# Staging tiles dealt out by hand, two chunks of attention moved later, and nine loads moved to GpSimd's queue

## Chip, cores and metric

The kernel runs on one core of one Trainium2 chip. The metric is the device time of one execution in microseconds. Before the change the median of 13 runs is 215.76 us (214.9 to 217.86).

In the profile PE is TensorE (PEld its weight loads), DVE is VectorE, ACT is ScalarE, POOL is GpSimd, and SP is SyncE, which issues DMAs here. A trailing q (SPq) means the sequencer's issue of a DMA.

## What is computed

A causal linear attention with a decay per head, in blocks, followed by a two-layer feed-forward network with SiLU. Batch 4, 8 heads, 768 positions, head size 64; 3072 tokens of width 512, hidden width 2048.

```python
# per batch and head, block by block
intra = (q_b @ k_b.T) * Dmask          # lam ** (i - j) where i >= j
out_b = intra @ v_b + (q_b * lam_pow) @ kv_state
kv_state = lam_block * kv_state + (k_b * rev_pow).T @ v_b
# then, on x = all heads side by side, 3072 x 512
h = x @ w_in                           # 512 x 2048
g = h * sigmoid(h)
y = g @ w_out                          # 2048 x 512
```

All inputs are float32; the matmuls run in bfloat16.

## The kernel before

**Tiles.** Tokens are cut into 24 chunks of 128 (six for a batch element) and ten groups of 256 or 384 tokens (`GROUPS`). Attention works by chunk, the network by group. For a chunk, queries and keys are scaled by powers of the decay while they are cast ("prep"), transposed, multiplied to scores, masked, and multiplied with the values; a running state `kv_ps` in PSUM is copied to `kvbd` for the next chunk. Keys and values are spread into block-diagonal tiles (`ktbd`, `vpad`, four of each) by DVE copies (`spread_k`, `spread_v`), so that two heads share one matmul. Chunk c uses buffer c mod 4.

**The start.** Chunks 0 to 3 (as two pairs, 0 and 2) and the up-projection of groups 0 and 1 follow a list written by hand, `ORDER`, whose words are carried out in turn by `table`. `kc`, `qc`, `vc` cast a half of a pair; `tk`, `tq` transpose on PE; `kt`, `qt` copy the transposes out of PSUM; `s` scores, `m` mask, `d` state update, `kv` state copy, `o` output, `x` copy of the output to `xt`, `w` cast of an input-weight piece, `u` and `g` up-projection and SiLU, `z` filler matmuls on a tile of zeros. A letter says which engine does it (A: ACT, D: DVE, P: POOL). Every engine works in the order of the program.

**Loads.** SP issues all large DMAs in program order. At the start these are 12 half pairs of chunks 0 to 3 (into tiles `pair`, six buffers that rotate), then the eight input-weight pieces W0 to W7 as 16 transfers of 256 KB into tiles borrowed from the `kf`, `vf` and `qf` rotations, then six output-weight pieces and the pair of chunk 4's queries into `pair` again, and so on. A later issue waits in SP's queue behind an earlier one.

**From chunk 6 on** keys and queries are transposed by DMA (`dma_t`, L373 and L374, on SP) after POOL's prep (L356 queries, L350 keys), and spread by DVE (L183). `next_prep` does this for the next chunk, and issues the loads of the chunk two further on (`load_c`, L232: queries, keys, values, 256 KB each in runs of 256 B). `piece(c, ...)` calls it until chunk c + 2 is prepared.

**The middle.** After the list, `down0` runs the down-projection of groups 0 and 1 with the attention of chunks 4 and 5 between its parts. Two calls of `next_prep` and the memsets of `clear_halves(0, 1)` (POOL; L198, L199) lie there. Then `stretch` interleaves, by positions between 0 and 1, the up-projection of one group (`ups`), the attention of the next group's chunks (`pieces`: scores, state, output for each) and the down-projection of the group before (`downs`). In the third group's stretch chunks 6 and 7 are placed from 0.2 to 1.15, chunk 6's keys are spread at 0.05, and half of the third group's down-projection comes at 1 to 1.5; the other half lies in the next stretch.

Of the kernel before, what the change touches and what calls it, by code (L numbers as in the profile page):

```python
# [12 lines left out]
BLK = 128  # L13
# [9 lines left out]
LOADS = "K00 Q00 K01 Q01 V00 V01 K20 Q20 K21 Q21 V20 V21 W0 W1 W2 W3 W4 W5 W6 W7"  # L23

ORDER = """
kc:0,0,A,u z:27 tk:0,0,att qc:0,0,D tq:0,0,h kc:0,1,D,s qt:0,0,D wl z:2 tk:0,1,att kt:0,1,A qc:0,1,P kt:0,0,D vc:0,0,D,s
z:4 s:0,0,h,att m:0,0,0,D vc:0,1,A,u tq:0,1,o z:1 d:0 m:0,0,1,D qt:0,1,A z:2 s:0,1,att,att kc:2,0,P,s kv:0,A m:0,1,1,D
m:0,1,0,D tk:2,0,h kt:2,0,D kc:2,1,A,u o:0,0,h,att qc:2,0,P qc:2,1,P x:0,0,A d:1 kv:1,A tq:2,0,o qt:2,0,D tk:2,1,o
kt:2,1,D o:0,1 x:1,1,A z:3 tq:2,1,h qt:2,1,D vc:2,0,A,u vc:2,1,P,s s:2,0,att,o m:2,0,1,D z:4 s:2,1,o,att m:2,0,0,D
m:2,1,1,D x:1,0,A m:2,1,0,D x:0,1,A w:0,1,D d:2 kv:2,A z:28 d:3 w:1,0,D o:2,0,o,att w:0,0,A o:2,1 x:2,0,D w:1,1,D w:2,0,D  # L30
kv:3,A x:2,1,D u:0,0,0,h,h x:3,0,D x:3,1,A w:3,1,D w:2,1,A w:3,0,D u:0,0,1 w:6,0,D g:0,0,1 g:0,0,0 w:5,0,D w:4,1,A
w:4,0,D u:1,1,0,o,o u:1,1,1 g:1,1,1 g:1,1,0 u:1,0,0,h,h u:1,0,1 g:1,0,0 g:1,0,1 w:7,0,D w:6,1,D w:5,1,A w:7,1,D
u:0,1,0,o,o u:0,1,1 u:0,2,0,h,h g:0,1,1 u:0,2,1 g:0,1,0 u:0,3,0,o,o u:0,3,1 g:0,2,0 g:0,2,1 u:1,3,0,h,h g:0,3,0 g:0,3,1
u:1,3,1 g:1,3,0 g:1,3,1 u:1,2,0,o,o u:1,2,1 g:1,2,1 g:1,2,0
# [4 lines left out]
def kernel(  # L39
# [72 lines left out]
    zero = const.tile([128, 256], BF16, name="zero")  # L112
# [33 lines left out]

    def w_piece(which, i, a, b):
        if which == "in":
            c, h = divmod(i, 2)
            return slice(2 * h + a, 2 * h + b), slice(512 * c, 512 * c + 512)  # L150
        return slice(2 * i + a, 2 * i + b), slice(0, DM)

    def load_w(which, *pieces):
        for i in pieces:
            if which == "in":
                for a in range(2):
                    ko, f = w_piece(which, i, a, a + 1)
                    n = 2 * i + a
                    tag = "qf" if n >= 12 else ("kf", "vf")[a]
                    t = io.tile([128, 1, 512], F32, name=tag, tag=tag, bufs=4 if tag == "qf" else 6)  # L160
                    nc.sync.dma_start(out=t, in_=w_in_r[:, ko, f])
                    wtmp[which, i, a] = t
            else:
                ko, f = w_piece(which, i, 0, 2)
                t = io.tile([128, 2, 512], F32, name="pair", tag="pair", bufs=6)
                nc.sync.dma_start(out=t, in_=w_out_r[:, ko, f])
                wtmp[which, i] = t

    def cast_w(which, i, e="D", part=None):
        a, b = (0, 2) if part is None else (part, part + 1)  # L170
        ko, f = w_piece(which, i, a, b)
        if which == "in":
            move(e, w_in_bf[:, ko, f], wtmp[which, i, part])
        else:
            move(e, w_out_bf[:, ko, f], wtmp[which, i][:, a:b, :])
# [30 lines left out]
    cell = {}  # L206
    start = 0
# [11 lines left out]
    def load_pair(src, c, dst, parts=((0, H),)):  # L219
        b, blk = divmod(c, NB)  # L220
        for lo, hi in parts:
            if c not in dst:
                dst[c] = io.tile([128, H, 2, D], F32, name="pair", tag="pair", bufs=6)
            nc.sync.dma_start(out=dst[c][:, lo:hi].rearrange("p h r d -> p h (r d)"),  # L224
                              in_=src[b, lo:hi, blk * BLK:(blk + 2) * BLK, :].rearrange("h (p r) d -> p h (r d)", r=2))
# [3 lines left out]
    def load_1(src, c, tag, bufs):  # L229
        b, blk = divmod(c, NB)  # L230
        t = io.tile([128, H, D], F32, name=tag, tag=tag, bufs=bufs)
        nc.sync.dma_start(out=t, in_=src[b, :, blk * BLK:(blk + 1) * BLK, :].rearrange("h s d -> s h d"))  # L232
        return t
# [12 lines left out]
    def pair_op(c, a, e, table, src, dst):  # L246
        hs = slice(4 * a, 4 * a + 4)
        src, dst = src[:, hs].rearrange("s h r d -> s r h d"), dst[:, :, hs, :]
# [8 lines left out]
    def op_c(raw, tiles, name, forward=False):  # L257
        def run(c, a, e, s="s"):
            if c not in tiles:
                tiles[c] = nat.tile([128, 2, H, D], BF16, name=name, tag=name, bufs=2)  # L260
# [3 lines left out]
    def op_t(src, name):  # L264
        def run(c, a, tag):
            tp = psum.tile([128, 2, 2, BLK], BF16, name=name, tag=tag, bufs=NBUF[tag], padded_shape=[128, 4, 2, BLK])
            for r in range(2):
                for p in range(2):
                    h = 4 * a + 2 * p
                    nc.tensor.transpose(tp[:, r, p, :], src[c][:, r, h:h + 2, :], ident)  # L270
# [3 lines left out]
    def op_tc(dst, name, of):  # L274
        def run(c, a, e):
            if c not in dst:
                dst[c] = nat.tile([128, 2, NP, BLK], BF16, name=name, tag=name, bufs=2)
            move(e, dst[c][:, :, 2 * a:2 * a + 2], cell.pop((of, c, a)))
# [4 lines left out]
    def op_s(c, a, *tags):  # L283
        sps = [psum.tile([128, 2, 2, 2, 64], F32, name="sp", tag=t, bufs=NBUF[t]) for t in tags]
        for r in range(2):
            for p in range(2):
                for j, x in ((0, 0), (1, 1), (0, 1), (1, 0)):
                    nc.tensor.matmul(sps[j][half[x], r, p], lhsT=ktp[c][half[j], r, 2 * a + p, half[x]],
                                     rhs=qtp[c][half[j], :, 2 * a + p, half[x]], start=True, stop=True)
# [8 lines left out]
    def op_o(c, a, *tags):  # L298
        if a == 0:
            for x, t in enumerate(tags):  # L300
                op_[c + x] = psum.tile([128, NP, 2, 64], F32, name="op", tag=t, bufs=NBUF[t])
        for x in range(2):
            if c + x > 0:
                for p in range(2):
                    nc.tensor.matmul(op_[c + x][:, 2 * a + p], lhsT=kvb[c + x][:, 2 * a + p, :],
                                     rhs=qtp[c][:, :, 2 * a + p, half[x]], start=(a == 0 and p == 0),
                                     stop=False, skip_group_check=True)
        for r in range(2):
            for p in range(2):
                for x, j in ((0, 0), (1, 1), (0, 1), (1, 0)):  # L310
                    nc.tensor.matmul(op_[c + x][half[j], 2 * a + p], lhsT=vp[c][half[x], r, 4 * a + 2 * p + j, :],
                                     rhs=ss_[c, a, j][half[x], r, p], start=(c + x == 0 and a == 0 and r == 0 and p == 0),
                                     stop=(r == 1), skip_group_check=True)

    def op_x(c, a, e):
        g, x = divmod(c, 2)
        if g not in xt:
            xt[g] = xpool.tile([128, KO_IN, GROUPS[g]], BF16, name="xt", tag="xt", padded_shape=[128, KO_IN, 512])
        ps = slice(2 * a, 2 * a + 2)
        move(e, xt[g].rearrange("d p (r x w) -> d p r x w", r=2, x=2)[:, ps, :, x, :], op_[c][:, ps])  # L320

    def op_d(c):
# [4 lines left out]
        for r in range(2):  # L327
            for p in range(NP):
                for j in range(2):
                    nc.tensor.matmul(kv[half[j], p, half[j]], lhsT=kp[c0][half[x], r, 2 * p + j, :],  # L330
                                     rhs=vp[c0][half[x], r, 2 * p + j, :], start=(c == 0 and r == 0 and p == 0), stop=True,
                                     skip_group_check=True)
# [3 lines left out]

    qpairs = {}
# [117 lines left out]
    def copy_kv(c, e="D"):  # L455
        if c % NB == NB - 1:
            return
        kv, kvs = kvps[c // NB], kvbd[c % NKV]
        for j in range(2):
            rows = slice(64 * j, 64 * j + 64)  # L460
            move(e, kvs[rows, :, rows], kv[rows, :, rows])
# [110 lines left out]
    def ffn2(g, mt, kos, tag="o"):  # L572
# [7 lines left out]
        if kos[-1] == KO_OUT - 1:  # L580
# [4 lines left out]
            if g < 2:  # L585
                dst = out[gstart[g]:gstart[g] + 256, :].rearrange("(q r) d -> q r d", r=2)[:, mt, :]
# [20 lines left out]
    for word in LOADS.split():  # L607
        if word[0] == "W":
            load_w("in", int(word[1]))
        else:  # L610
            a = int(word[2])
            src, dst = {"Q": (q, rawq), "K": (k, rawk), "V": (v, vraw)}[word[0]]
            load_pair(src, int(word[1]), dst, ((4 * a, 4 * a + 4),))
    load_w("out", *range(6))
    load_q(4)
    load_k(4), load_k(5)
    load_w("out", 6, 7)
    load_v(4), load_v(5)
    load_c(6)
    load_c(7)  # L620

    def op_u(g, b, h, *tags):
        for i, tag in zip((2 * b, 2 * b + 1), tags):
            ffn1_open(g, i, tag)
        for i in (2 * b, 2 * b + 1):
            ffn1_mm(g, i, range(2 * h, 2 * h + 2))  # L630

    def op_g(g, b, i):
        ffn1_close(g, 2 * b + i)
# [4 lines left out]
    def op_z(n):  # L638
        if 0 in kvps:
            for i in range(n):  # L640
                nc.tensor.matmul(kvps[0][half[0], NP - 1, half[1]], lhsT=zero[:, half[0]], rhs=zero[:, half[0]],  # L641
                                 start=False, stop=True, skip_group_check=True)
        else:
            wt = psum.tile([128, NP, BLK], F32, name="warm_ps", tag="kv", bufs=1)
            for i in range(n):
                nc.tensor.matmul(wt[:, 0:2], lhsT=zero[:, :BLK], rhs=zero, start=True, stop=True)
# [7 lines left out]
    for word in ORDER.split():  # L654
        name, _, args = word.partition(":")
        table[name](*[int(a) if a.isdigit() else a for a in args.split(",") if a])

# [4 lines left out]
    def next_prep():  # L662
        c = state["prepped"]
        if c < NCHUNK:
# [4 lines left out]
            if loads:  # L669
                load_c(loads.pop(0))  # L670
# [3 lines left out]
    for i in range(6):  # L674
        cast_w("out", i)
    for i in range(NKV):
# [28 lines left out]
    next_prep()  # L705
    down0(3, 0)
    st_o(5)
    next_prep()
# [36 lines left out]
    def stretch(*parts):  # L745
# [3 lines left out]
        for _, _, _, (fn, *args) in sorted(units, key=lambda u: u[:3]):  # L749
            fn(*args)  # L750

    stretch((ups(2), 0, 1), ([(vcast, 6)], 0.0, 0.1), ([(spread_k, 6)], 0.05, 0.05), ([(spread_v, 6)], 0.3, 0.3), (pieces(3), 0.2, 1.15),
            (downs(2, range(1)), 1, 1.5))
    for g in range(3, len(GROUPS)):
        parts = [(ups(g), 0, 1), (pieces(g + 1), *((0.1, 0.95) if g == 3 else (0, 0.85)))]
        parts.append((downs(g - 1, range(1 if g == 3 else 0, nch[g - 1])), 0, 1))
# [34 lines left out]
```

## Time and profile before

| | us |
|---|---|
| median of 13 runs | 215.76 |
| the profiled execution | 215.65 |
| its span on the core | 213.9 |
| PE busy | 203.1 (95%) |
| DVE busy | 116.6 |
| ACT busy | 98.4 |
| POOL busy | 53.4 |

The span runs from the first instruction to the last; 1.75 us of the profiled execution's time lie around it. Busy time is the union of an engine's instructions, without DMA issues. The granted TensorE clock is full in all slices. The views used below are the list of waits (who waited for whom, total, number of times, longest), the timeline (start, duration, engine, line, what was written from what, count; the idle time before and what ended it in brackets) and the groups of instructions by line.

### The profile page before, as it was taken

Reading aid. Unit: us, or ns where it says so; the run is one execution under the profiler, and the core shown is the slowest. Engines: PE = TensorE matmul, PEld = TensorE weight load, DVE = VectorE, ACT = ScalarE, POOL = GpSimd, SP = SyncE. Lnnn points to the kernel's source line nnn. Section 1 sums busy time; section 2 is a strip of 40 time slices with the busy share of each in tenths; the row PEclk is TensorE's granted clock in tenths of the full one; section 3 lists DMA queues with packets and bytes.
Section 4 is the critical chain, followed back from the end, with each engine's and each line's share of the span. In section 5 each row is a group of like instructions: output and inputs, shape, how many; then the busy total and the mean of one; then the engine's idle time right before and its main releaser. Section 6 shows DMA issues by size and latency. Waiting matters only on the chain.

```text
span 213.9 us, 4591 instructions
## 1 busy us (share of the span) xinstructions
PE 203.1 (95%) x1808; PEld 135.2 (63%) x1831; DVE 116.6 (54%) x263; ACT 98.4 (46%) x186; POOL 53.4 (25%) x66
## 2 busy tenths in 40 slices
PE   7679999999799999999999999999999999999994
PEld 6467886556677777776665655556655565566654
DVE  3787447597785679854992785345461351110121
ACT  3973863415463564545555445445445334423210
POOL 6360002449433334321333332212000000000000
PEclk9999999999999999999999999999999999999999
DMA  4999999989899999989888999858411011011112
GB/s 113 334 364 326 394 405 270 316 195 199 195 285 204 223 201 193 213 204 202 174 223 196 235 207 182 196 165 174 124 49 52 2 49 54 0 49 49 52 49 98
DMA packets 95670, 38.58 MB, mean 180 GB/s; under 512 B 81056, under 2 KB 88608, under 8 KB 95648
## 3 DMA queue, kind: packets, MB, share of 16 engines
q1 hardware_dynamic: 95504, 38.29, 70.1%
q8 instruction: 14, 0.23, 0.5%
q14 instruction: 8, 0.07, 0.1%
q10 hardware_dynamic: 144, 0.00, 0.0%
HBM read 27.27 MB, written 6.29 MB: 157 GB/s over the span
## 4 chain that ended last, share of the span: by engine, by line
PE 88%; SPq 3%; DVE 2%; DMA 2%; issue 1%; POOL 1%; ACT 1%; POOLq 0%
PE o_ps L578 36%; PE h_ps L552 19%; PE h_ps L529 18%; PE op L507 5%; PE sp L476 3%; SPq L224 3%; DMA pair<-in_q_dram 2%; PE kv_ps L452 2%; PE o_part L595 2%; DVE ktbd L183 1%; DVE xt L183 1%; POOL vp L253 0%; PE kv_ps L641 0%; POOL qb L253 0%; ACT kvbd L179 0%
## 5 line engine op out<-in xcount | busy, mean ns | idle before, releaser
L578 PE MATMUL o_ps<-w_out_bf,g 128*128 128x512 bf16 x345 | 87.9, 379 | 1.2
L578 PEld LDWEIGHTS <-g 128*128 128x128 bf16 x368 | 35.0, 98 | 30.8
L556 ACT ACTIVATE g<-h_ps 128x384 bf16<-128x384 f32 x64 | 31.4, 491 | 46.6 <-PE h_ps L552 46.1
L552 PE MATMUL h_ps<-xt,w_in_bf 128*128 128x384 bf16 x256 | 50.6, 326 | 0.0
L529 PE MATMUL h_ps<-xt,w_in_bf 128*128 128x256 bf16 x384 | 47.2, 273 | 0.7 <-ACT w_in_bf L179 0.7
L534 ACT ACTIVATE g<-h_ps 128x512 bf16<-128x512 f32 x48 | 27.8, 596 | 33.2 <-PE h_ps L529 33.0
L529 PEld LDWEIGHTS <-w_in_bf 128*128 128x128 bf16 x384 | 36.4, 98 | 7.9 <-ACT w_in_bf L179 1.1
L582 DVE COPY ob<-o_ps 128x512 f32<-128x512 f32 x23 | 15.9, 691 | 44.1 <-PE o_ps L578 44.0
L356 POOL TENSOR_TENSOR qb<-qf,lam_fwd 128x512 bf16<-128x512 f32 x18 | 18.9, 1053 | 68.1 <-DMA qf<-in_q_dram 64.3
L552 PEld LDWEIGHTS <-w_in_bf 128*128 128x128 bf16 x256 | 23.7, 98 | 17.2
L483 DVE TENSOR_TENSOR ss<-sp,mask 128x512 bf16<-128x512 f32 (+1 forms) x40 | 21.0, 566 | 14.6 <-PE sp L476 14.4
L387 DVE COPY vpad<-vb 64x256 bf16<-64x256 bf16 x72 | 25.3, 351 | 1.6
L350 POOL TENSOR_TENSOR kb<-kf,lam_bwd 128x512 bf16<-128x512 f32 x20 | 20.9, 1048 | 1.4 <-DMA kf<-in_k_dram 0.9
L183 DVE CAST kvbd<-kv_ps 64x256 bf16<-64x256 f32 x32 | 13.5, 421 | 9.7 <-PE kv_ps L452 9.4
L515 ACT ACTIVATE xt<-op 128x512 bf16<-128x512 f32 x20 | 11.9, 597 | 12.7 <-PE op L507 12.0
L183 DVE COPY ktbd<-kn 64x512 bf16<-64x512 bf16 x36 | 14.3, 396 | 5.0 <-DMA kn<-kb 4.6
L476 PEld LDWEIGHTS <-ktbd 128*128 128x128 bf16 x160 | 9.4, 98 | 5.5 <-DVE ktbd L183 2.3
L476 PE MATMUL sp<-qt,ktbd 128*128 128x128 bf16 (+1 forms) x160 | 10.3, 207 | 1.8 <-DVE ktbd L183 1.8
L179 ACT ACTIVATE vb<-vf 128x512 bf16<-128x512 f32 x18 | 11.2, 622 | 0.0
L507 PE MATMUL op<-ss,vpad 128*128 128x128 bf16 (+1 forms) x160 | 10.3, 207 | 0.0
L507 PEld LDWEIGHTS <-vpad 128*128 128x128 bf16 x160 | 8.9, 98 | 0.3
L183 DVE CAST w_out_bf<-pair 128x1024 bf16<-128x1024 f32 x7 | 5.5, 780 | 4.7 <-DMA pair<-in_moe_w_out_dram 4.7
(83 smaller groups left out, 119.7 us busy)
## 6 DMA issues: line engine op xcount, KB each, us to landing
out_dram<-ob SPq DMA_DIRECT2D x23, 256.0 KB, 3.4
kf<-in_k_dram SPq DMA_DIRECT2D x20, 256.0 KB, 4.0
vf<-in_v_dram SPq DMA_DIRECT2D x20, 256.0 KB, 4.3
qf<-in_q_dram SPq DMA_DIRECT2D x18, 256.0 KB, 3.3
pair<-in_moe_w_out_dram SPq DMA_DIRECT2D x8, 512.0 KB, 7.7
kf<-in_moe_w_in_dram SPq DMA_DIRECT2D x6, 256.0 KB, 5.4
vf<-in_moe_w_in_dram SPq DMA_DIRECT2D x6, 256.0 KB, 5.6
pair<-in_k_dram SPq DMA_DIRECT2D x4, 256.0 KB, 4.5
```

Source lines behind the costliest of these rows:

```text
L183: nc.vector.tensor_copy(dst, src)
L350: VG[e].tensor_tensor(kb, rawk.pop(c).rearrange("s (p j) d -> s p j d", j=2), decay(lam_bwd, c % NB), op=AL.mult)
L356: nc.gpsimd.tensor_tensor(qb, rawq.pop(c).rearrange("s (p j) d -> s p j d", j=2), decay(lam_fwd, c % NB), op=AL.mult)
L387: nc.vector.tensor_copy(vh[64 * j:64 * j + 64, :, h, j, :], vb[64 * h:64 * h + 64, :, j, :])
L476: nc.tensor.matmul(sp[:, p, :], lhsT=lhsT, rhs=qt[:, p, a:], start=True, stop=True)
L483: VG[e].tensor_tensor(ss, sp, m[:, None, :n].to_broadcast([128, 4, n]), op=AL.mult)
L507: nc.tensor.matmul(dst, lhsT=lhsT, rhs=rhs, start=(i == 0), stop=(i >= len(terms) - NP), skip_group_check=True)
L529: nc.tensor.matmul(hps[g, i][:, a:a + 256], lhsT=w_in_bf[:, ko, m * 128:(m + 1) * 128], rhs=xt[g][:, ko, :], start=(ko == 0 and u == 0), s ...
L534: nc.scalar.activation(gg.rearrange("p u n -> p (u n)"), hps[g, i], AF.Silu)
L552: nc.tensor.matmul(hp[:, a:z], lhsT=w_in_bf[:, ko, m * 128:(m + 1) * 128], rhs=xt[g][:, ko, a:z], start=(ko == 0 and a == 0), stop=(ko == ...
L556: nc.scalar.activation(gg, hp[:, :n], AF.Silu)
L578: nc.tensor.matmul(o, lhsT=gt[g, ko][:, mt * BLK:(mt + 1) * BLK], rhs=w_out_bf[:, ko, :], start=(ko == 0), stop=(ko == KO_OUT - 1))
```

## The change

Five things change together.

1. *Staging.* The rotating `pair` tiles become six tiles dealt out in turn by `next_pair`. Input-weight pieces 0 to 5 are loaded as one transfer of 512 KB into them, pieces 6 and 7 into two `kf` and two `vf` tiles. Their loads are no longer issued all together after the inputs: a list `later` issues each as soon as the words of `ORDER` that read its tile are in the program, so that on SP they stand behind the waits for those casts.
2. *The list.* `ORDER` is new. Chunk 2's second half is attended after the up-projection has begun; the state update and its copy can be done by halves (`d:2,0`). Fillers are not instructions in a tile of their own: after the first ones, `z` leaves a number that the next `s`, `o` or `u` writes into its own PSUM tile ahead of its matmuls, with up to 512 columns each.
3. *Layout and width.* Groups 0 and 1 share one tile `xall`, in the order of the tokens; from the second quarter of the hidden width on, their up-projection is done together with 512 columns. The state update takes two heads in one matmul. The stores of groups 0 and 1 are plain rows.
4. *Chunks 6 and 7.* Both are prepared and transposed before the last quarter of `down0`, the loads of chunks 8 and 9 follow after that, and their attention moves from 0.2..1.15 to 0.8..1.9 of the third group's stretch, with the whole down-projection of that group from 1 to 2.
5. *Queue.* The loads of chunks 8, 9 and 10 are issued by GpSimd and not by SP.

The core of the diff:

```diff
-LOADS = "K00 Q00 K01 Q01 V00 V01 K20 Q20 K21 Q21 V20 V21 W0 W1 W2 W3 W4 W5 W6 W7"
+LOADS = "K00 Q00 K01 Q01 V00 V01 K20 Q20 K21 Q21 V20 V21"
 ORDER = """
+kc:0,0,D,u z:20 tk:0,0,h qc:0,0,D kt:0,0,A wl z:8 tq:0,0,o kc:0,1,D,s qt:0,0,A z:2 tk:0,1,h qc:0,1,D z:3 tq:0,1,o
+s:0,0,h,att vc:0,1,A,u vc:0,0,D,s d:0 kt:0,1,D m:0,0,1,D m:0,0,0,D qt:0,1,A kv:0,A s:0,1,att,att qc:2,0,P z:2 o:0,0,h,o
+kc:2,0,A,u m:0,1,0,D m:0,1,1,D x:1,0,D d:1 qc:2,1,P tk:2,0,att tq:2,0,h x:0,0,A kt:2,0,D o:0,1,att,att tq:2,1,o
+kc:2,1,A,u tk:2,1,h qt:2,0,A x:1,1,D x:0,1,D kt:2,1,D vc:2,0,P,s s:2,0,o,h kv:1,A d:2,0 qt:2,1,A vc:2,1,P,s z:2
+s:2,1,att,att m:2,0,0,D m:2,0,1,D kv:2,0,A d:2,1 w:0,1,D kv:2,1,D m:2,1,1,D w:1,1,D o:2,0,h,att m:2,1,0,D w:0,0,A
+u:0,0,0,o,o x:2,0,A d:3 w:1,0,A kv:3,A x:3,0,D u:0,0,1 g:0,0,1 w:2,0,D o:2,1,att,att x:3,1,D x:2,1,A g:0,0,0 w:2,1,D
...
+    pairs = [const.tile([128, 2 * H * D], F32, name=f"pair{i}") for i in range(6)]
...
+            ko, f = w_piece(which, i, 0, 2)
+            t = next_pair().rearrange("p (k f) -> p k f", k=2)
+            nc.sync.dma_start(out=t, in_=(w_in_r if which == "in" else w_out_r)[:, ko, f])
...
+        e = nc.gpsimd if c in (8, 9, 10) else nc.sync
+        e.dma_start(out=t, in_=src[b, :, blk * BLK:(blk + 1) * BLK, :].rearrange("h s d -> s h d"))
...
+        for m in ms:
+            for ko in range(2 * h, 2 * h + 2):
+                nc.tensor.matmul(hps["m", m], lhsT=w_in_bf[:, ko, m * 128:(m + 1) * 128], rhs=xall[0][:, :, ko, :],
+                                 start=(ko == 0), stop=(ko == KO_IN - 1))
...
+        while later and not later[0][2]:
+            load_w(*later.pop(0)[:2])
...
     st_d(5)
-    next_prep()
+    next_prep(0)
+    next_prep(2)
     down0(3, 0)
     st_o(5)
-    next_prep()
     clear_halves(0, 1)
     down0(3, 1)
...
-    stretch((ups(2), 0, 1), ([(vcast, 6)], 0.0, 0.1), ([(spread_k, 6)], 0.05, 0.05), ([(spread_v, 6)], 0.3, 0.3), (pieces(3), 0.2, 1.15),
-            (downs(2, range(1)), 1, 1.5))
+    stretch((ups(2), 0, 1), ([(vcast, 6)], 0.0, 0.1), ([(spread_k, 6)], 0.5, 0.5), ([(spread_v, 6)], 0.6, 0.6),
+            (pieces(3), 0.8, 1.9), (downs(2, range(2)), 1, 2), ([(next_prep,)], 0.6, 0.6))
     for g in range(3, len(GROUPS)):
         parts = [(ups(g), 0, 1), (pieces(g + 1), *((0.1, 0.95) if g == 3 else (0, 0.85)))]
-        parts.append((downs(g - 1, range(1 if g == 3 else 0, nch[g - 1])), 0, 1))
+        if g > 3:
+            parts.append((downs(g - 1, range(nch[g - 1])), 0, 1))
         stretch(*parts)
```

The argument of `next_prep` is the number of chunks whose loads it issues after preparing one.

## Prediction

> **What bounds the kernel now.** I read the page's busy row first: PE is busy for 203.1 of 213.9 us, so time is won only by taking idle time or work out of PE, or lost by making PE wait. The rate tells that the busy time is real: 111 matmuls of 256 columns run from 21.82 to 33.95 us, 0.109 us each, and four of 512 columns take 0.86 us in the chain. The list of waits of PE (total, times, longest) is short:
>
> ```profile
> PE sp L476 <- DVE ktbd L183: 1.8, 1, 1.8
> PE tk L270 <- ACT kp L179: 1.6, 1, 1.6
> ...
> PE kv_ps L641 <- ACT kvbd L179: 0.9, 1, 0.9
> PE h_ps L529 <- ACT w_in_bf L179: 0.7, 1, 0.7
> PE tk L270 <- POOL kp L253: 0.4, 1, 0.4
> ```
>
> One wait, 1.8 us, lies in the dense part: the scores of chunk 6. The others lie before 22 us. The timeline shows the 1.8 us and what stands in front of it (start, duration, engine):
>
> ```profile
> 49.94 0.95 POOL L198 MEMSET ktbd<- 128x1024 bf16 x1
> ...
> 51.92 2.83 DVE L183 COPY ktbd<-kn 64x512 bf16<-64x512 bf16 x2
> ...
> 54.81 0.51 PE L476 MATMUL sp<-qt,ktbd 128*128 128x128 bf16 x8 [1.78 <-DVE ktbd L183]
> ```
>
> The two copies that spread chunk 6's keys take 2.83 us beside POOL's memsets (a pair takes 0.59 at 58.73), and PE stands until 54.81. After that PE is never late, but by little. The SP timeline says why: SP issues transposes, loads and stores one behind the other, without a gap:
>
> ```profile
> 46.99 1.48 SPq L373 DMA_TRANSPOSE qt<-qb  x1
> 48.57 1.21 SPq L374 DMA_TRANSPOSE kn<-kb  x1
> 49.83 0.57 SPq L232 DMA_DIRECT2D qf<-in_q_dram  x1
> 50.46 0.68 SPq L232 DMA_DIRECT2D kf<-in_k_dram  x1
> 51.24 0.66 SPq L232 DMA_DIRECT2D vf<-in_v_dram  x1
> 51.99 0.86 SPq L570 DMA_DIRECT2D out_dram<-ob  x1
> 52.95 1.24 SPq L373 DMA_TRANSPOSE qt<-qb  x1
> ```
>
> A chunk costs SP 2.6 us of transposes and 2.1 us of loads. The spread of chunk 10 ends at 78.36 and its scores start at 78.42; for chunk 14 it is 101.83 and 102.22. So a gain ahead of these chunks stays only if their keys come earlier too.
>
> **The start (order, wide matmuls, staging).** The up-projection starts at 18.97 now. In the new order it follows `o:2,0` and the casts of the first weight piece. POOL gets four tiles of chunk 2: the second query half landed at 12.43 (its row starts on the DMA), then 1.04 each: 13.47, 14.51, 15.55. State update `d:2,1` follows at 15.6, and `o:2,0` ends near 16.5. The first weight piece was cast at 16.24 and 16.73; DVE is free of chunk 2's masks at about 15.8, ACT at 15.4, so I put both casts' end at 16.9 and the first up-projection at 17.0. Behind it stand 32 matmuls of 256 columns (3.5 us), 48 of 512 (10.4) and the attention that was moved behind the start (`d:3`, `o:2,1`: 1.2 from their rows of 0.44 and 0.82): the end is 32.0 instead of 33.95, **1.9 us** earlier. Width alone gives 96 x 0.109 - 48 x 0.215 = 0.1 of this.
>
> The weight loads must now wait for the casts that empty their staging tile, the last on `vc:2,1` (15.55). It costs nothing while earlier loads are in flight: pieces 0 to 4 are issued by 13.5, and the trace moves such a piece in about 1.3 us behind inputs that land until 13.9, so DMA has work until 20. Without that cover each late piece would hold the weights behind it in SP's queue. Fewer fillers (37 units of 256 columns, against 34 and 37 tiny ones) take nothing from the sum; they ran in waits.
>
> Then a DMA is late next: the last output-weight piece lands at 40.49 (ACT idle 5.25 us for it), its cast takes 1.06 and the query copy behind it 0.54, so chunk 4's scores can't start before 42.1; PE would be there at 41.55. That leaves **1.35 us**: the third group starts at 51.12 - 1.35 = 49.75.
>
> **Chunks 6 and 7 later.** Their scores move from 0.2 of the third group to 0.89 of it, 6.1 us in, at 55.9. The keys had landed by 51.92, so the **1.78 us** go. Both chunks now lie between eight units of the down-projection, which are only brought forward from the next stretch. Possible gain: 1.35 + 1.78 + rounding = 3.2 us. Next due, by counting units of 0.87 (up), 0.86 (down) and 1.1 (a chunk's attention): chunk 8 at 66.6, chunk 9 at 71.2, chunk 10 at 75.0.
>
> **Loads 8 to 10 from GpSimd.** SP loses 9 issues of 0.57 to 0.68, some 6 us, which is why its transposes of chunks 8 to 10 need not be late. POOL gets them in its own row of work: prep 6, prep 7, six loads, the four memsets, prep 8, three loads, prep 9, prep 10. Prep 7 ends at 50.0 (it waits for its landing at 47.95). Let one issue hold POOL for t. Memsets (four starts 0.89 apart, 3.7 with the last) and prep 8 (2.1) end at 55.8 + 6t; three loads and prep 9 end at 57.9 + 9t; SP's transposes of chunk 9 take 2.6, load 11 takes 2.1, then the transposes of chunk 10: 1.3 to the second issue, 2.4 to its landing (its median), 0.6 spread. **Chunk 10 is ready at 66.9 + 9t and due at 75.0.** Chunks 8 (60.1 + 6t against 66.6) and 9 (62.2 + 9t against 71.2) are parts of the same loss. Change: -3.2 + (9t - 8.1), the bracket not below 0. Zero at t = 1.26.
>
> The trace has no DMA issued by POOL. Lower bound: SP's issue of the same load, 0.57 (full gain; POOL need not be slower). Upper: the longest issue of such a load, 3.19 (+17.4). Nearest are POOL's own passes: 1.04 for one 128x512 tile; a transfer has 1024 pieces of 256 B to describe, on a reading and a writing side, so one pass to two, 1.04 to 2.08. I take 1.5 as an estimate between these: 9 x 1.5 - 8.1 = 5.4, and -3.2 + 5.4 = +2.2.
>
> DVE copies held up beside POOL show a second price: the copies `ktbd<-kn` have a median of 291 ns and a maximum of 1782. The Trainium skill, "SBUF — State Buffer", section "SBUF: two separate sides", says that GpSimd and a two-port DVE copy lock each other out for a whole instruction, and that a DMA issued from GpSimd can't write its descriptors meanwhile; that would make t longer, no row here shows it. "DMA: Bandwidth & Descriptors", "Specifications", gives about 1 us to the first byte by GpSimd and 0.6 by sync; if 1 us were all of t, the estimate by that page would be -2.3. Its section "Issuing engines are not separate DMA queues" says that other engines save only issue time; here issue time is what SP lacks, so the rule doesn't refute the change, but it names no other gain.
>
> **Rivals.**
> 1. *Forecast, 0.37:* t from 1.33 to 2.2, POOL's queue becomes the bound for chunks 8 to 10; 216.3 to 224.
> 2. *A cheap issue, 0.33:* t up to 1.2. At 0.57 chunk 10 is ready at 72.0 and all 3.2 us stay, 212.5; at 1.04 1.3 us are lost, 213.8. For it: POOL is 25% busy and idles up to 5 us before a prep. Against it: SP's hardware already needs 0.57.
> 3. *A dear issue, 0.21:* t above 2.2: at 2.4 +10.3, 226; at 3.19, 233.
> 4. *Break-even, 0.09:* t near 1.26, or the change doesn't do what it says: the start gains nothing because the weights decide it as before (DVE waited for them until 23.69), or fewer fillers slow the transposes. Then 1.78 is the whole gain and due times come 1.35 later; below t = 1.05 the time is 214.0, above it the sum is as before, since the chain of chunk 10 doesn't move with PE. So a wrong first half moves little.
>
> **Numbers.** The profiled execution took 215.65 with a span of 213.9, so 1.75 lie around it, which I keep; the median of the runs is 0.11 higher. 215.65 + 2.2 + 0.1 = 218.0. The likeliest case's own range is 216.3 to 224. Range of eighty per cent: from the full gain, 212.4, to t = 2.4, 226.0. A measurement can tell some 0.3% from no change; faster (rival 2 and a little of 4) 0.34, same 0.08, slower 0.58.
>
> **What would show it.** Right: PE's wait list has no wait for `ktbd` at chunk 6, the down-projection starts near 32, and there are new waits of `sp` for `ktbd` between 66 and 82, with POOL solid from 48 to about 73. POOL's issue rows give t directly. Wrong: rows of POOL near 0.6 to 1.0 (faster), a first up-projection at 18 or later, or spreads that wait for DVE rather than for prep.

## The result and the profile after

The changed kernel takes **218.14 us** (median of 11 runs, 216.95 to 219.61); the kernel before, run beside it, 215.66. The ratio is **1.0119, 95% interval [1.0092, 1.0146]**. All ratios leave out, on both sides, runs over 1.5% above the fastest of their kernel. The profiled execution took 217.72 with a span of 216.0, against 215.65 and 213.9. Lines of the code have moved: the scores are L492, the output L523, the mask L499, the up-projection L545 (512 columns wide: L645), the down-projection L594, DVE's moves L187, the spread of the values L401, POOL's preps L370 and L364, its memsets L202 and L203.

The list of waits of PE (total, times, longest):

```profile
PE op L523 <- DVE ss L499: 2.1, 1, 2.1
PE sp L492 <- DVE ktbd L187: 2.1, 3, 1.4
...
PE o_ps L594 <- ACT g L654: 0.7, 1, 0.7
...
PE h_ps L545 <- DVE xt L187: 0.6, 1, 0.6
```

One wait for `ktbd` has become three, and there is a new one for the masks. PE's timeline says at which chunks (start, duration; the wait in brackets):

```profile
57.80 0.51 PE L492 MATMUL sp<-qt,ktbd 128*128 128x128 bf16 x8 [1.41 <-DVE ktbd L187]
...
63.22 0.61 PE L523 MATMUL op<-ss,vpad 128*128 128x128 bf16 x8 [2.08 <-DVE ss L499]
...
65.85 0.51 PE L492 MATMUL sp<-qt,ktbd 128*128 128x128 bf16 x8 [0.30 <-DVE ktbd L187]
71.59 0.50 PE L492 MATMUL sp<-qt,ktbd 128*128 128x128 bf16 x8
76.21 0.50 PE L492 MATMUL sp<-qt,ktbd 128*128 128x128 bf16 x8
79.95 0.50 PE L492 MATMUL sp<-qt,ktbd 128*128 128x128 bf16 x8
...
91.19 0.51 PE L492 MATMUL sp<-qt,ktbd 128*128 128x128 bf16 x8 [0.36 <-DVE ktbd L187]
```

Chunks 6 and 7 are late, the very chunks that were moved to be early. Chunks 8, 9 and 10 (71.59, 76.21, 79.95), whose loads POOL issues, wait for nothing. DVE's timeline shows where the time of chunk 6 is:

```profile
50.93 6.82 DVE L187 COPY ktbd<-kn 64x512 bf16<-64x512 bf16 x2
57.78 4.66 DVE L401 COPY vpad<-vb 64x256 bf16<-64x256 bf16 x4
62.47 1.02 DVE L499 TENSOR_TENSOR ss<-sp,mask 128x512 bf16<-128x512 f32 x2
```

The keys were there in time, since the copy began at 50.93 and PE got to the scores at 56.39. But the two key copies take 6.82 us (median of all such copies 0.29 each), the four value copies 4.66 (0.22 each). The first key copy alone ran from 50.93 to 56.70, one value copy for 2.35 from 58.98 to 61.33. The masks stand behind them in DVE's queue, and so the output at 63.22. That order is new: in the kernel before, the masks of chunk 6 (55.32) came ahead of its value copies (56.26), and the fourth part put the values first. Now POOL's row over the same time:

```profile
50.28 0.88 POOL L246 DMA_DIRECT2D qf<-in_q_dram  x1
51.16 0.88 POOL L246 DMA_DIRECT2D kf<-in_k_dram  x1
52.03 0.88 POOL L246 DMA_DIRECT2D vf<-in_v_dram  x1
52.91 0.97 POOL L202 MEMSET ktbd<- 128x1024 bf16 x1
...
55.59 0.97 POOL L203 MEMSET vpad<- 128x1024 bf16 x1
56.51 1.09 POOL L370 TENSOR_TENSOR qb<-qf,lam_fwd 128x512 bf16<-128x512 f32 x1
...
60.39 0.88 POOL L246 DMA_DIRECT2D vf<-in_v_dram  x1
61.29 1.06 POOL L370 TENSOR_TENSOR qb<-qf,lam_fwd 128x512 bf16<-128x512 f32 x1
```

The row has no gap. The first copy ends at 56.70, just after the last memset (56.56), the long value copy at 61.33, just after the last issue (61.27). The loads themselves cost POOL 0.88 to 1.06 each, which is the t of the prediction.

**The account** is of the two profiled executions. A wait costs 0.16 more than the list says, because the modelled duration of the eight matmuls before a dense stretch (0.51) is that much longer than the time to the next start (57.80 to 58.15, 0.35). The third group starts 1.00 earlier (50.12 against 51.12); the old wait saves 1.78 + 0.16 = 1.94; the new ones cost 1.57 + 2.24 + 0.46. Sum +1.33; measured at the scores of chunk 10, 79.95 - 78.42 = +1.53. With chunk 12's 0.52 it is +1.85; measured at chunk 13, 97.96 - 95.91 = +2.05, which stays to the end (span +2.1). Some 0.2 before chunk 10 is not assigned.

### The profile page after: what moved, and what is told of

It reads as the page before. It is cut to its first block, busy times and chain, and to the rows that moved or that the text cites. A ratio compares the mean times of both kernels' runs of the same rounds, so it can differ in the third digit from the quotient of the medians.

```text
span 216.0 us, 4342 instructions
## 1 busy us (share of the span) xinstructions
PE 203.8 (94%) x1677; PEld 127.8 (59%) x1700; DVE 123.4 (57%) x267; ACT 98.7 (46%) x185; POOL 61.0 (28%) x74
## 4 chain that ended last, share of the span: by engine, by line
PE 83%; DVE 7%; issue 2%; DMA 2%; ACT 2%; SPq 2%; DVEq 0%
PE o_ps L594 34%; PE h_ps L568 19%; PE h_ps L545 11%; PE h_ps L645 5%; DVE ktbd L187 5%; PE op L523 5%; PE sp L492 3%; DMA pair<-in_v_dram 2%; PE o_part L609 2%; SPq L237 2%; PE kv_ps L466 2%; DVE vpad L401 1%; PE kv_ps L344 1%; ACT kvbd L183 1%; ACT qtp L183 1%
## 5 line engine op out<-in xcount | busy, mean ns | idle before, releaser
L594 PE MATMUL o_ps<-w_out_bf,g 128*128 128x512 bf16 x346 | 88.1, 379 | 1.8 <-ACT g L654 0.7
L594 PEld LDWEIGHTS <-g 128*128 128x128 bf16 x368 | 34.9, 98 | 31.8 <-issue 1.0
L545 PE MATMUL h_ps<-xt,w_in_bf 128*128 128x256 bf16 x288 | 36.0, 273 | 0.6 <-DVE xt L187 0.6
L370 POOL TENSOR_TENSOR qb<-qf,lam_fwd 128x512 bf16<-128x512 f32 x18 | 18.8, 1047 | 61.9 <-DMA qf<-in_q_dram 61.9
L568 PEld LDWEIGHTS <-w_in_bf 128*128 128x128 bf16 x256 | 23.7, 98 | 17.2
L550 ACT ACTIVATE g<-h_ps 128x512 bf16<-128x512 f32 x36 | 21.4, 597 | 27.3 <-PE h_ps L545 27.1
L499 DVE TENSOR_TENSOR ss<-sp,mask 128x512 bf16<-128x512 f32 (+1 forms) x40 | 21.0, 566 | 17.1 <-PE sp L492 16.8
L545 PEld LDWEIGHTS <-w_in_bf 128*128 128x128 bf16 x288 | 27.1, 98 | 6.1 <-issue 0.5
L187 DVE COPY ktbd<-kn 64x512 bf16<-64x512 bf16 x36 | 23.7, 658 | 0.4
L401 DVE COPY vpad<-vb 64x256 bf16<-64x256 bf16 x72 | 21.3, 296 | 1.6
L364 POOL TENSOR_TENSOR kb<-kf,lam_bwd 128x512 bf16<-128x512 f32 x20 | 21.8, 1091 | 1.6 <-DMA kf<-in_k_dram 1.6
L187 DVE CAST kvbd<-kv_ps 64x256 bf16<-64x256 f32 (+1 forms) x34 | 14.0, 413 | 9.7 <-PE kv_ps L466 9.4
L492 PEld LDWEIGHTS <-ktbd 128*128 128x128 bf16 x160 | 9.3, 98 | 6.3 <-DVE ktbd L187 3.3
L492 PE MATMUL sp<-qt,ktbd 128*128 128x128 bf16 (+1 forms) x160 | 10.3, 207 | 2.2 <-DVE ktbd L187 2.1
L523 PE MATMUL op<-ss,vpad 128*128 128x128 bf16 (+1 forms) x160 | 10.4, 207 | 2.1 <-DVE ss L499 2.1
L523 PEld LDWEIGHTS <-vpad 128*128 128x128 bf16 x160 | 8.9, 98 | 2.8 <-issue 1.7
L645 PE MATMUL h_ps<-xt,w_in_bf 128*128 128x512 bf16 x48 | 10.5, 379 | 0.0
```

The costliest lines, as they stand in the source:

```text
L187: nc.vector.tensor_copy(dst, src)
L364: VG[e].tensor_tensor(kb, rawk.pop(c).rearrange("s (p j) d -> s p j d", j=2), decay(lam_bwd, c % NB), op=AL.mult)
L401: nc.vector.tensor_copy(vh[64 * j:64 * j + 64, :, h, j, :], vb[64 * h:64 * h + 64, :, j, :])
L492: nc.tensor.matmul(sp[:, p, :], lhsT=lhsT, rhs=qt[:, p, a:], start=True, stop=True)
L499: VG[e].tensor_tensor(ss, sp, m[:, None, :n].to_broadcast([128, 4, n]), op=AL.mult)
L523: nc.tensor.matmul(dst, lhsT=lhsT, rhs=rhs, start=(i == 0), stop=(i >= len(terms) - NP), skip_group_check=True)
```

## The experiments

All ratios are to the kernel before, run on the same chip in the same set.

**First set: what holds the copies?** The theory: POOL's unbroken row. The rivals: SP or the landing of the keys, and POOL's queue being late for chunks 8 to 10.

`e1_loads_on_sp`: the change without its fifth part.

```diff
-        e = nc.gpsimd if c in (8, 9, 10) else nc.sync
-        e.dma_start(out=t, ...)
+        nc.sync.dma_start(out=t, ...)
```

> The changed kernel with the nine loads of chunks 8 to 10 back on SP; POOL keeps the four memsets. Held copies (a DVE copy from SBUF to SBUF can't run while POOL works without a gap, as from 47.5 to 61.3 us in the changed kernel): POOL is done with the memsets near 51.1, so the two key copies of chunk 6 end before 52, the waits of 1.41 and 2.08 us at chunk 6 and of 0.30 at chunk 7 go, and the time is 218.1 - 4.3 = 213.8 or a little less. Late queue (what the prediction held: POOL reaches the preps of chunks 8 to 10 too late): the rows of the changed kernel show its issues at 0.9 us, so the queue costs nothing and putting the loads back gives 218, at most 0.5 less. Late data (the new start makes the data of chunks 6 and 7 late): 218, the waits stay.

Measured: 215.47 (12 runs), ratio 0.9957 [0.9916, 0.9998]. The row of memsets now lies from 47.84 to 51.47, before the keys are spread, and DVE's timeline of this run has

```profile
51.42 0.58 DVE L187 COPY ktbd<-kn 64x512 bf16<-64x512 bf16 x2
52.03 0.94 DVE L400 COPY vpad<-vb 64x256 bf16<-64x256 bf16 x4
```

So copies of the same form are short again, and chunk 6 waits for nothing. Chunk 10's scores start at 76.10, 2.3 earlier than before the change. But two new waits follow, at chunks 11 and 12, the time misses the 213.8 of the theory, and at chunk 13 (95.77) 0.1 of the gain is left:

```profile
83.67 0.51 PE L491 MATMUL sp<-qt,ktbd 128*128 128x128 bf16 x8 [1.06 <-DVE ktbd L187]
89.00 0.51 PE L491 MATMUL sp<-qt,ktbd 128*128 128x128 bf16 x8 [0.78 <-DVE ktbd L187]
```

So the fifth part is what holds the copies. In this run its relief of SP is missed too: without it, chunks 11 and 12 are late. SP transposes the keys of chunk 11 only at 78.67, after a set of loads and a store, and they land 4.3 us later, those of chunk 12 at 85.70, 2.6 us. Whether they are late in every such run, `e4_sp_and_clear_on_dve` puts in doubt.

`e2_clear_on_dve`: the loads stay on GpSimd, the four memsets go to DVE.

```diff
-            nc.gpsimd.memset(ktbd[i], 0.0)
-            nc.gpsimd.memset(vpad[i], 0.0)
+            nc.vector.memset(ktbd[i], 0.0)
+            nc.vector.memset(vpad[i], 0.0)
```

> The changed kernel with the loads of chunks 8 to 10 on POOL, but the four memsets done by DVE (4 x 0.5 us, from about 50.5 to 52.5). Held copies: POOL's unbroken row shrinks by 3.6 us; the first key copy ends behind the sixth issue near 53, the second near 54, so the wait at the scores of chunk 6 (due 56.2) goes, while the value copies may still be held by the issues for chunk 10, 0 to 1.5 us at chunk 6's output; 214.5 (213.8 to 216). If it is the DMA issues alone that hold the copies: as here, 214.5. If it is the memsets alone: 213.8 and no copy longer than 0.5 us. Late data: 218.

Measured: six runs, one of 214.17 and five of 218.17 to 219.67, so there is no ratio; the trace is of a run of 218.66. In it the first key copy lasts from 52.75 to 54.02, to the end of the six issues (53.90): issues alone hold a copy too. The second takes 2.10, beside two preps. Chunks 6 and 7 don't wait, but chunk 8 does, for 3.02, because its keys' transpose landed 13.2 us after its issue (56.52 to 69.7) in place of 2.4. DVE's timeline names that as the cause of its idle time:

```profile
69.79 0.89 DVE L187 COPY ktbd<-kn 64x512 bf16<-64x512 bf16 x2 [4.55 <-DMA kn<-kb]
```

Whether the run of 214.17 escaped that, no trace shows.

`e3_chunk6_on_act`: chunk 6's spreads on ACT.

```diff
-                move_k("D", c, j, kn)
+                move_k("A" if c == 6 else "D", c, j, kn)
```

(and so for the values)

> The changed kernel, all of POOL's work as it is, but the six copies that spread chunk 6's keys and values run on ACT instead of DVE (some 0.6 us for a key copy, 0.4 for a value copy, 2.8 in all, in a stretch where ACT idles 0.28 us per SiLU). Held copies: ACT isn't held by POOL, so the waits of 1.41 and 2.08 us go; up to 1 us may come back where SiLU is late for PE; 214.5 (213.8 to 215.5). Late data: the copies on ACT wait as long as those on DVE did, 217.5 to 218.5. Late queue: 218.

Measured: 217.26 against the 214.5 expected, ratio 1.0065 [1.0029, 1.0100]. Chunk 6's scores no longer wait for keys. But chunk 7's copies, still DVE's, now meet POOL's second row (key copies from 62.26, 3.40 us), its scores wait 1.44, and PE waits 1.7 for SiLU results behind the copies on ACT. The hold moved with the place, as it must if the row makes it.

`e4_sp_and_clear_on_dve`: the edits of `e1_loads_on_sp` and `e2_clear_on_dve` together.

> The changed kernel with the loads of chunks 8 to 10 on SP and the four memsets on DVE, so that POOL has only preps. Held copies: all waits of chunks 6 and 7 go, 213.8 as with the loads on SP alone, within 0.5 (the memsets then cost 2 us of DVE where it has slack). Late data or late queue: 218. If SP's queue is what the loads were moved away from, new waits for keys appear at chunks 8 to 10 and the time is above 214.5.

Measured: 215.72, ratio 0.9965 [0.9921, 1.0008], with runs from 212.94 to 216.57; the interval reaches 1, and the 213.8 expected is missed. In the profiled one (214.15) the only waits for `ktbd` are 0.33 (chunk 9) and 0.26 (chunk 14), and chunk 10's scores are at 76.55. Chunks 11 and 12 don't wait here, though the loads are on SP as in `e1_loads_on_sp`: the keys of chunk 11 are transposed at 78.16 and land in 2.6. How much of that is the memsets' place and how much differs from run to run isn't shown.

**Second set: the form of the copy, and each part alone.**

`e5_two_input`: the changed kernel, chunks 6 and 7 spread by DVE with another operation of the same result (the core of the edit; it is done for these two chunks alone).

```diff
-nc.vector.tensor_copy(dst, src)
+nc.vector.tensor_tensor(dst, src, src, op=AL.max)
```

> The changed kernel, but the spreads of chunks 6 and 7 (keys and values) are DVE operations with two inputs, the larger of a tile and itself, in place of copies with one input; the values written are the same, the engine and the place in its queue too. Theory (POOL's unbroken row of issues and memsets holds a DVE copy of SBUF to SBUF in its one-input form): the first of chunk 6's key operations no longer takes 5.77 us but under 1, PE's waits of 1.41 and 2.08 at chunk 6 and 0.30 at chunk 7 go, and the time is 218.1 - 3.5 = 214.6; 2.2 of these should show at chunk 10, whose scores then start near 77. Rival (whatever DVE writes to SBUF is held while POOL is busy, in any form): the operations still take over 3 us and the time stays within 217 to 219. Rival 2 (the keys themselves are late and the copy's duration is only where it shows): the waits stay, and the operations begin later.

Measured: ratio **0.9938 [0.9887, 0.9989]**, from four runs of 214.12 to 215.71; the profiled one took 214.22. Five others took 217.40 to 218.88, and no trace tells why; a late landing as in `e2_clear_on_dve` isn't excluded there. In the profile no score waits for `ktbd` (chunk 7's output waits 0.43 for its masks), and chunk 10's scores are at 76.45 (expected near 77). DVE's timeline:

```profile
51.39 0.84 DVE L411 TENSOR_TENSOR ktbd<-kn 64x512 bf16<-64x512 bf16 x2
52.27 1.20 DVE L411 TENSOR_TENSOR vpad<-vb 64x256 bf16<-64x256 bf16 x4
...
61.20 2.34 DVE L411 TENSOR_TENSOR vpad<-vb 64x256 bf16<-64x256 bf16 x4
```

The first two lines run beside the six issues (48.63 to 54.06 here), which are part of the row that held the copy for 5.77 us, and are not held. The third runs beside issues until 62.31 and then POOL's prep (62.33), and takes twice as long. So the one-input copy was held by issues (`e2_clear_on_dve`) and by memsets (the kernel before), and the two-input form was not held by issues; beside memsets alone no run has it. Next to a prep, which reads SBUF, it is slowed too. The Trainium skill, "SBUF — State Buffer", section "SBUF: two separate sides", has this distinction: an exclusive lock between GpSimd and a DVE operation in a two-port mode, or one with two SBUF inputs only against a GpSimd operation that reads SBUF. The rows agree with that, though none shows the port or the mode of a copy. They differ in one point: the page speaks of the length of one instruction, and here a copy was held over seven that followed one another without a gap (5.77 us).

`e6_before_pool`: the kernel before with the fifth part alone (the `e = nc.gpsimd ...` lines of the diff above).

> The kernel before with one edit alone: the nine loads of chunks 8 to 10 are issued by GpSimd. Its staging, list and the places of chunks 6 and 7 are the old ones. Theory (POOL's row holds the DVE copies): six issues of 0.9 us now stand between prep 6 and the memsets, so POOL is busy without a gap from about 47 to 60, chunk 6's first key copy takes 5 us or more in place of 2.2, and the wait of 1.78 at chunk 6 grows by 3 to 5.3, not all of which is given back: 217.5 to 221. Rival (the prediction's step: chunks 8 to 10 late by POOL's queue): no change at chunk 6, a wait at chunk 10. Rival 2 (SP's relief is worth something by itself): faster, 214 to 215, because transposes of chunks 8 to 10 come earlier.

Measured: 221.52 (4 runs), ratio **1.0254 [1.0205, 1.0303]**. The wait is where and as large as expected, but not for the expected reason. (The first key copy took 1.78 in the kernel before, not 2.2.) PE's line, then DVE's:

```profile
58.56 0.82 PE L477 MATMUL sp<-qt,ktbd 128*128 128x128 bf16 x8 [5.67 <-DVE ktbd L183]
```

```profile
57.16 1.34 DVE L183 COPY ktbd<-kn 64x512 bf16<-64x512 bf16 x2 [5.29 <-DMA kn<-kb]
```

The copies are short; DVE idled 5.29 us for the transpose. Grouped by tile over 44 to 60 us, the transposes of chunks 6 and 7 are from issue to landing (min, median, max), first in this run, then in `e1_loads_on_sp`:

```profile
DMA to landing us min/median/max: 8.9/9.1/9.3
```

```profile
DMA to landing us min/median/max: 2.3/2.4/2.4
```

In the kernel before itself, over the same time:

```profile
DMA to landing us min/median/max: 3.0/3.7/4.4
```

In this run the first two loads of chunk 8 are issued (46.08, 47.13) ahead of the transpose of chunk 6's keys (47.76); from SP's queue all three would follow it. Whether that or the hold decides, `e9_before_pool_two` below tells.

`e7_before_part4`: the kernel before with the fourth part alone (new places of chunks 6 and 7, `next_prep(0)`, `next_prep(2)`).

> The kernel before with the fourth part alone: chunks 6 and 7 prepared together and attended from 0.8 to 1.9 of the third group's stretch, the whole down-projection of that group there, loads of chunks 8 to 10 on SP. Theory: the wait of 1.78 at chunk 6 goes and nothing takes its place before chunk 10: 215.7 - 1.9 = 213.8. Rival (as with the loads on SP in the changed kernel, the gain is lost again because SP's transposes of chunks 11 and 12 come no earlier): a new wait of sp for ktbd between 83 and 90, together 1 to 1.9, and 215.0 to 215.7.

Measured: 217.08, ratio 1.0066 [1.0030, 1.0102]. Chunk 6's wait goes, and later ones take its place:

```profile
77.59 0.51 PE L476 MATMUL sp<-qt,ktbd 128*128 128x128 bf16 x8 [1.03 <-DVE ktbd L183]
85.61 0.51 PE L476 MATMUL sp<-qt,ktbd 128*128 128x128 bf16 x8 [1.51 <-DVE ktbd L183]
```

These are chunks 10 and 11, and the output of chunk 11 waits 0.88 more for its masks; the rival was right in kind, but named chunks 11 and 12 and was too mild in size. SP is busy without a gap ahead of them (the keys of chunk 10 are transposed at 74.45, after loads and a store; those of chunk 11 at 80.07, and they land 4.9 us later).

`e8_start_only`: the first three parts alone, with loads on SP and the old middle.

> The changed kernel with only its first three parts (staging, list, layout and width): chunks 6 and 7, the preparation and the down-projection are as before, loads of chunks 8 to 10 on SP. Theory: the third group starts at 50.1 in place of 51.1, but chunk 6's keys are spread by POOL's and SP's times, which hardly move, so the wait at its scores grows from 1.78 to about 2.8 and the time stays near 215.6. Rival (the start's gain is PE's and stays): the wait stays 1.8, and 214.7.

Measured: 215.14, ratio 0.9963 [0.9933, 0.9992]. Both theories missed: the wait at chunk 6 shrank from 1.78 to 0.48, because the earlier start brought the memsets forward too (the last ends at 51.74) and the key copies, from 51.41, took 1.53 in place of 2.83. Chunk 10 is 1.8 earlier; waits of 0.52 at chunk 12 and 0.31 at chunk 14 take part of it back, and the end is 0.4 earlier.

**Third set: what delays the transposes, and a better version.**

`e9_before_pool_two`: `e6_before_pool` with the two-input spreads of `e5_two_input`.

> The kernel before with the nine loads of chunks 8 to 10 on GpSimd (the run that waited 5.67 at chunk 6), and with the spreads of chunks 6 and 7 as two-input DVE operations (the larger of a tile and itself). It tells two causes of that 5.67 apart. Theory now: the keys' transposes landed late (9.1 us after their issue in that run, 2.4 to 2.9 with the loads on SP), because the loads on GpSimd's queue stand in front of them in the DMA engines; then the two-input form changes little, the key operations again start near 57, the wait stays 4.5 to 5.7 and the time is 220 to 221.5. Rival (POOL's row holds the copies, as in the changed kernel, and the late landing is only where the profile puts it): the operations start near 51 and the wait falls to about 1, 216 to 217.

Measured: 222.26, ratio 1.0299 [1.0254, 1.0345]. The form changes nothing here: DVE's line

```profile
58.15 1.60 DVE L398 TENSOR_TENSOR ktbd<-kn 64x512 bf16<-64x512 bf16 x2 [6.24 <-DMA kn<-kb]
```

shows the operation beginning late, and PE waits 6.88. So the loads on GpSimd's queue have a second price, the late landing of transposes that are issued while they are under way. That they stand in front of them in the DMA engines was not seen directly, but fits: the late ones were issued after the first such loads, while in the changed kernel chunk 6's transpose (46.25, landed in 2.4) was issued before them (47.47). The next three there came after them and landed in 4.4, 7.1 and 4.9, late too, but no score waited for them. The Trainium skill, "DMA: Bandwidth & Descriptors", section "Issuing engines are not separate DMA queues", says that DMAs of all issuers run on the same engines and interleave; 9.1 against 2.4 us agrees with that. One thing leaves a doubt: in both runs the late keys of chunk 6 land within 0.2 us of the end of POOL's memsets (57.21 and 58.25), so that POOL's row itself delays the landing isn't excluded; the landings of chunk 7's keys, 60.3 and 61.4, show no such meeting.

`e10_load10`: the changed kernel, only chunk 10's loads on GpSimd, memsets on DVE, two-input spreads for chunks 6 and 7 (the first of the three edits):

```diff
-        e = nc.gpsimd if c in (8, 9, 10) else nc.sync
+        e = nc.gpsimd if c == 10 else nc.sync
```

> The changed kernel with three edits: only the loads of chunk 10 are on GpSimd (8 and 9 on SP), the four memsets are on DVE, and the spreads of chunks 6 and 7 are two-input operations. Theory: POOL's row no longer holds a spread; transposes of chunks 8 and 9 land in 2.4 as with all loads on SP; SP is relieved of 2 us just before the transposes of chunks 11 and 12, which were late by 1.06 and 0.78 with all loads on SP; so the waits at chunks 6 to 12 stay under 0.4 together and the time is 213.3 to 214.3. Rival (three loads on GpSimd are enough to put transposes behind them in the DMA engines): a wait of 1 us or more at chunks 8 to 10, 215 to 216.

Measured: **214.38** (9 runs, 213.66 to 215.65), ratio **0.9921 [0.9887, 0.9956]**, the lowest of all, though its interval overlaps those of `e1_loads_on_sp`, `e4_sp_and_clear_on_dve`, `e5_two_input` and `e8_start_only`. The one wait for `ktbd` in PE's list is 0.3, at chunk 12, and the key transposes land in 2.6 us (median of those issued from 40 to 90; the longest 4.4). Three edits were made at once, so what each is worth isn't shown.

`e11_act_queue`: the changed kernel, loads of chunks 8 to 10 from ACT's queue, memsets on DVE.

```diff
-        e = nc.gpsimd if c in (8, 9, 10) else nc.sync
+        e = nc.scalar if c in (8, 9, 10) else nc.sync
```

> The changed kernel with the loads of chunks 8 to 10 issued from ACT's queue in place of GpSimd's and the four memsets on DVE; the spreads are one-input copies again. Theory: nothing of POOL's stands beside the copies but the preps, so they take under 1.6 us; ACT pays nine issues of about 0.6 us, some 5.5 us between 47 and 61, where it is busy for 1.0 to 2.3 of each 3 us, so some SiLU results come up to 1 us later; if the loads overtake transposes in the DMA engines as they do from GpSimd, a wait of 1 to 3 us shows at chunk 8 or 9, as with the memsets on DVE and the loads on GpSimd: 214.5 to 217. Rival (ACT's issues hold nothing up and the transposes land in time): 213.5 to 214.3.

Measured: 224.83, ratio 1.0414 [1.0354, 1.0474]. Neither case: the sixth load was issued only at 56.97, after a wait, and on ACT everything waits behind it. PE's list of waits and ACT's timeline:

```profile
PE h_ps L545 <- ACT xt L531: 7.5, 1, 7.5
```

```profile
51.70 2.03 ACTq L246 DMA_DIRECT2D kf<-in_k_dram  x1
56.97 0.38 ACTq L246 DMA_DIRECT2D vf<-in_v_dram  x1
57.39 0.60 ACT L531 ACTIVATE xt<-op 128x512 bf16<-128x512 f32 x1 [8.62 <-DMA kf<-in_k_dram]
```

The copy to `xt` that the next up-projection reads came after 8.62 us without work on ACT. The profile names the landing of the key load before it as what ended that; why the sixth issue had to wait for it isn't shown.

## Why the prediction was right in number and wrong in its step

The forecast of 218.0 met 218.14 by luck: two errors, of 5.4 and 4.3 us, nearly cancelled.

- **The start.** First up-projection at 17.0 forecast, 16.25 measured; down-projection at 32.0 forecast (its terms add up to 32.1), 32.96 measured, with 0.69 of waiting for SiLU there, 0.55 for `xt` and other short gaps not counted. The last output-weight piece, named as late next, landed at 38.78 and not 40.49, and didn't bind. Gain 1.00 against 1.35 in this profile, and it is the largest of those with this start: chunk 4's scores come at 42.48 here and at 42.73 to 43.29 in the eight others, at 43.34 to 43.60 in the four with the old start. Half a us is nearer to what the start is worth. `e8_start_only` shows that a gain reaches chunk 10 and is then mostly given back.
- **Chunk 6 later.** The 1.78 was booked as gone because "the keys had landed by 51.92". Landing was not the condition; the copies were. In the profile before they had taken 2.83, beside four memsets, and the change put six issues ahead of the memsets, into the place where the copies now lie. **This is the step that failed**: the lines were shown, "a second price" was named, and no term of the sum was given to it. It measured 1.57 + 2.24 + 0.46 = 4.3 us, the 2.24 by way of the masks, which the new order has behind the value copies.
- **Loads 8 to 10 from GpSimd.** t was taken as 1.5; it is 0.88 to 1.06. By the prediction's own chain chunk 10 is then ready by 76.4 at the latest and the bracket 9t - 8.1 at most 1.4, where 5.4 was booked. Measured, it is 0: chunks 8 to 10 wait for nothing, in `e5_two_input` too, where the hold delays PE by 0.43 at most. The case named as likeliest did not occur; by t it was the second, a cheap issue, whose time of 212.5 to 213.8 did not come because of the copies.
- **The sum.** Forecast -1.35 - 1.78 + 5.4; measured -1.00 - 1.94 + 4.3, then 0.5 at chunk 12 and 0.2 not assigned. A term that wasn't there (5.4) and one that was left out (4.3) nearly cancelled.
- **The signs.** The first, no wait for `ktbd` at chunk 6, failed. POOL was solid, but from 45.5 to 65.3 and not "from 48 to about 73". New waits of the scores for `ktbd` "between 66 and 82" were wrong: they came at 57.80, 65.85 and 91.19. Rows of POOL "near 0.6 to 1.0" came, but not the speed that they were to bring. "Spreads that wait for DVE rather than for prep" was listed as a sign of error, and what came is nearest to that: spreads that began in time and were held on DVE.
- **Relief of SP.** Right as a need in two profiles: with the loads on SP chunks 11 and 12 wait 1.84 (`e1_loads_on_sp`), and chunks 10 and 11 2.54 with the fourth part alone (`e7_before_part4`). In the profile of `e4_sp_and_clear_on_dve` they don't wait, so its size isn't settled.

The parts, each by itself: start (the first three) 0.9963, later attention 1.0066, queue 1.0254; the first four together 0.9957, all five 1.0119. The queue costs 1.6% on top of the first four, and 2.5% on the kernel before, where it hits a transpose and not a copy.

## What to carry to other kernels

Before work is put on GpSimd, look at what DVE does beside it: a copy whose maximum is several times its median may already be held, and a longer unbroken row on GpSimd can stretch that hold to its own end, as it did here from 1.78 to 5.77 us for one copy. Moving a load to another engine's queue also takes it out of its order: it may overtake a transfer that is needed sooner, and whatever stands behind an issue that waits, waits too. A total that comes out right says nothing about its terms; check each against its row.

## What was not expected of the hardware

- A one-input bf16 copy on DVE, 64x512, was held 5.77 us over three DMA issues and four memsets of GpSimd in a row (median 0.29); a two-input operation on the same tiles took 0.42 beside such issues.
- A load of 256 KB in runs of 256 B costs GpSimd 0.88 to 1.06 us to issue, and SP mostly 0.5 to 1.1.
- During the 5.67 us in which PE stood still, the granted clock fell to half, and it stayed there for some microseconds after. Windows of `e6_before_pool` (us; busy time and instructions of PE, PEld, DVE, ACT, POOL; granted clock; DMA share; GB/s):

```profile
53.00:56.00 3.00, 0.00 (x0) 0.00 (x0) 0.00 (x0) 1.04 (x2) 3.00 (x4) 0.91 1.10 167
56.00:59.00 3.00, 0.44 (x5) 0.45 (x6) 1.32 (x2) 0.00 (x0) 3.00 (x4) 0.50 1.01 207
59.00:62.00 3.00, 3.00 (x20) 2.14 (x19) 2.68 (x5) 0.60 (x1) 3.00 (x4) 0.50 1.03 371
```

The sixteen matmuls behind the scores took 3.40 us there and 1.91 in the kernel before. Chunk 6's scores are 3.75 later than before (58.56 against 54.81), chunk 7's 5.36 (64.74 against 59.38): the wait cost 1.6 us more than its length. In the changed kernel, whose longest wait after the start is 2.1, the granted clock stayed full; after the wait of 3.02 in `e2_clear_on_dve` it was 0.51 in the mean of the next 3 us.
